# Two chunks of a retention kernel change places, four of their loads move to ScalarE's queue, and half of a block of gates moves ahead of the last output weights

## The chip, the cores and the metric

The kernel runs on one core of a Trainium2 chip. Its time is the device time of one execution in microseconds; the median of nine executions is given where nothing else is said. Lower is better.

## The reference

Causal retention over 8 sequences of 576 tokens with 8 heads of 64, and behind it a gated feed-forward layer on the 4608 tokens that come out.

```python
scores = (1 / sqrt(D)) * q @ k.T                          # per batch and head
gamma  = 1 - 2 ** (-5 - arange(H));  rel = pos[:, None] - pos[None, :]
ret    = scores * where(rel >= 0, gamma ** rel, 0)
x      = (ret @ v)                                        # then heads side by side: [4608, 512]
out    = (sigmoid(x @ w_gate) * (x @ w_val)) @ w_out      # 512 -> 1536 -> 512
```

## The kernel before

The sequences are cut into chunks of 128 tokens; the fifth chunk of each sequence has 64. There are 40 chunks, numbered from 0 in the order of tokens. Chunks 0 to 3 are done in pairs at the very start. Each later chunk s goes through these steps: its k, q and v are loaded (`load`), cast on GpSimd, called POOL here (`cast_k`, `cast_q`, `cast_v`, with the decay in the tables), turned by TensorE (`turn`, for chunks 4 and 5) or by a DMA transpose (`cross`, from chunk 6 on) into the tile `T`, and attended: a score step `qk` (L427) masked on VectorE (`pt`, L429), two state steps `st0` and `st1` (L460) whose sum VectorE copies to `sbd` (L466), and `pv` (L446, L448), which ScalarE copies into `xT` (L450). Chunk 4, `PAIRED`, is the short last chunk of sequence 0: it has `qk` and `pv` alone and uses the state that the pairs left. Chunk 5 is the first of sequence 1 and needs no earlier state. So neither depends on the other. `cast_dense` makes a second copy of v on ScalarE for the state steps.

The feed-forward layer runs over blocks of tokens. `h_units` makes, for each of 12 pieces `fc` of the 1536 hidden columns, the gate and value products on TensorE (L524), the sigmoid on ScalarE (`g`) and the product on VectorE (`gv`). Then `gv` times the output weights `wo_sb` gives `op`. A block of at most 256 tokens takes several pieces to one bank of PSUM; the banks come from a list given by the caller.

The change lies in the first 70 us, where the weights themselves are still being loaded. The first block is tokens 0 to 511 (`h_first`, called for each piece), with the four output banks `opps` and the 48 matmuls of L746; then comes the block of tokens 512 to 639, made of chunk 4 (64 tokens) and half of chunk 5. Both are written out by hand, and calls of `advance` put the attention steps of the list `order` between the matmuls. From token 640 on a loop does this by a count of columns.

Every engine works through its instructions in the order in which the program issues them, and so does SyncE's queue of loads. All loads go through 18 buffers `ld`; the list `freed` says by hand which earlier buffer a new load takes over. In the queue before stand the two pairs, the gate and value weights, chunks 4 and 5, output weights 0 to 7, chunk 6, output weights 8 to 11, chunk 7, and so on. `cast_wo(f, engine)` casts output weight f on the engine given; the cast waits for its load, and what is behind it on that engine waits too. Chunk 4 is loaded by six DMAs, two for each of k, q and v, one for the even and one for the odd heads on 64 partitions each.

Of the kernel before, what the change touches and what calls it, by code (L numbers as in the profile page):

```python
# [9 lines left out]
FP32 = mybir.dt.float32  # L10
# [6 lines left out]
def kernel(  # L17
# [59 lines left out]
    freed += [(nm, 0, i) for nm in "gv" for i in range(2)] + [("g", f, i) for f in (2, 4) for i in range(2)]  # L77
    freed += [("v", 2, 0), ("v", 2, 1), ("v", 4, 0), ("g", 6, 0), ("v", 4, 1), ("g", 6, 1), ("v", 6, 0), ("g", 8, 0),
              ("v", 6, 1), ("g", 8, 1), ("g", 10, 0), ("v", 8, 0), ("g", 10, 1), ("v", 8, 1), ("v", 10, 0), ("v", 10, 1)]
    freed += [("k", 4), ("q", 4), ("v", 4), ("o", 0), ("k", 5), ("o", 1), ("q", 5), ("o", 2), ("o", 3), ("o", 4), ("o", 5),  # L80
              ("o", 6), ("v", 5)] + [("o", f) for f in range(7, NFC)]
    for s in range(6, NS):
        freed += [("k", s), ("q", s)] + ([("v", s - 2)] if s > 7 else [])
    slot = {}
# [1 line left out]
    def ld_tile(shape, key):  # L86
        n = len(slot)
        slot[key] = n if n < SLOTS else slot[freed[n - SLOTS]]
        return ld_pool.tile(shape, FP32, tag=f"ld{slot[key]}", name="_".join(["ld"] + [str(x) for x in key]))
# [8 lines left out]
    def bank(psum, tag, shape, name, dt=FP32):  # L98
        if psum is ffn_psum:
            return ffn_bank(shape, name, dt)  # L100
        return psum.tile(shape, dt, tag=tag, name=name)

    def load(s):
        b, c = STEPS[s]
        n = width[c]
        t0 = c * P
        tiles = []
        for nm, src in (("k", k), ("q", q), ("v", v)):
            if s == PAIRED:

                t = ld_tile([P, M, D], (nm, s))
                for e in range(2):
                    nc.sync.dma_start(out=t[e * 64:e * 64 + 64], in_=src[b, e::2, t0:t0 + n, :].rearrange("m p d -> p m d"))
                tiles.append(t)
                continue
            t = ld_tile([P, H, D], (nm, s))
            nc.sync.dma_start(out=t[0:n], in_=src[b, :, t0:t0 + n, :].rearrange("h p d -> p h d"))  # L117
            tiles.append(t)
        loaded[s] = tiles

    def load_pair(A):
# [19 lines left out]
    def load_wo(f):  # L141
        t = ld_tile([P, DM], ("o", f))
        nc.sync.dma_start(out=t, in_=moe_w_out[f * P:(f + 1) * P, :])
        parts["o", f] = t
# [2 lines left out]
    load_pair(1)  # L147
    for f in range(0, NFC, 2):
        load_w(f, 2)
    load(4)  # L150
    load(5)
    for f in range(NFC):
        if f == 8:
            load(6)
        load_wo(f)
    LEAD_CAST = 3


# [31 lines left out]
    qtab, ktab = tables([P, NC, H, 1], [[P, NC], [1, 1]], 1, lambda t, h: t[:, :, h, :])  # L190
    qtab = qtab.rearrange("p c h o -> p c (h o)")
    ktab = ktab.rearrange("p c h o -> p c (h o)")

    qtab4, ktab4 = [consts.tile([P, M], FP32, name=nm) for nm in ("qtab4", "ktab4")]
    for t4, t in ((qtab4, qtab), (ktab4, ktab)):
        for hh in range(2):
            nc.vector.tensor_copy(out=t4[hh * 64:hh * 64 + 64], in_=t[0:64, NC - 1, hh::2])
    warm = consts.tile([P, 1], FP32)
    nc.scalar.activation(out=warm, in_=lnscale, func=AF.Sigmoid)

# [36 lines left out]
    def cast_wo(f, eng):  # L237
        eng(out=wo_sb[:, f, :], in_=parts.pop(("o", f)))
# [19 lines left out]
    def cast_k(s):  # L258

        b, c = STEPS[s]  # L260
        n = width[c]
        k32 = loaded[s][0]
        kn = qk_nat[s % NB][:, 1:3]
        for j in range(n // 64):
            for hh in range(2):
                nc.gpsimd.tensor_tensor(  # L266
                    out=kn[half(hh), j, :, half(hh)], in0=k32[half(hh)] if s == PAIRED else k32[half(j), hh::2, :],
                    in1=(ktab4[half(hh)] if s == PAIRED else ktab[half(j), c, hh::2]).unsqueeze(2).to_broadcast([64, M, D]),
                    op=ALU.mult)
        natural["k", s] = kn  # L270

    def cast_q(s):
        b, c = STEPS[s]
        n = width[c]
        q32 = loaded[s][1]
        if s == PAIRED:
            for hh in range(2):
                nc.gpsimd.tensor_tensor(
                    out=qk_nat[s % NB][0:n, 0, :, half(hh)], in0=q32[half(hh)],
                    in1=qtab4[half(hh)].unsqueeze(2).to_broadcast([64, M, D]), op=ALU.mult)  # L280
            return
        qs = qk_nat[s % NB][:, 0].rearrange("p m (hh d) -> p (m hh) d", d=D)
        nc.gpsimd.tensor_tensor(out=qs[0:n], in0=q32[0:n],  # L283
                                in1=qtab[0:n, c, :].unsqueeze(2).to_broadcast([n, H, D]), op=ALU.mult)

    def cast_v(s):

        b, c = STEPS[s]
        n = width[c]
        v32 = loaded[s][2]  # L290
        vb = vbd[s % NB]
        for j in range(n // 64):
            for hh in range(2):
                nc.gpsimd.tensor_copy(out=vb[half(hh), j, :, half(hh)],  # L294
                                      in_=v32[half(hh)] if s == PAIRED else v32[half(j), hh::2, :])
        natural["vb", s] = vb

    def cast_dense(s, j):
# [17 lines left out]
    def turn(s, engs):  # L316

        nb = 1 + width[STEPS[s][1]] // 64
        t = att_pool.tile([P, 3, M, P], BF16, tag="T", name=f"T_{s}", bufs=4)
        for b0, eng in zip(range(0, nb, 2), engs):  # L320
            n = min(2, nb - b0)
            ps = qk_psum.tile([P, n, M, P], BF16, tag="qk", name=f"Tp_{s}_{b0}")
            for i in range(n):
                for m in range(M):
                    nc.tensor.matmul(ps[:, i, m, :], lhsT=qk_nat[s % NB][:, b0 + i, m, :], rhs=ident,
                                     is_transpose=True, start=(i == 0 and m == 0), stop=(i == n - 1 and m == M - 1))
            eng(out=t[:, b0:b0 + n], in_=ps)
        turned["q", s] = t[:, 0]
        turned["k", s] = t[:, 1:3]

    turned = {}

# [5 lines left out]
    def half(x):  # L338
        return slice(x * 64, x * 64 + 64)
# [129 lines left out]

    order = []  # L470
    for s in range(PAIRED, NS):
        if STEPS[s][1] < NC - 1:
            order += [("st0", s), ("qk", s), ("st1", s), ("pv", s)]
        else:
            order += [("qk", s), ("pv", s)]
# [8 lines left out]
    def casts_to(s):  # L484
        while done["cast"] <= min(NS - 1, s):
            x = done["cast"]
            loads_to(x + (1 if x < 16 else 2))
            cast_k(x)
            cast_q(x)
            cross(x)  # L490
            cast_v(x)
            done["cast"] += 1

    def run_phase(kind, s):
        if kind == "qk":
            casts_to(s + LEAD_CAST)
            phase_qk(s)
            if s > 5:
                cast_dense(s + 1, 0)
        elif kind == "pv":  # L500
            phase_pv(s)
            if s > 5:
                cast_dense(s + 1, 1)
        else:
            phase_st(s, int(kind[2]))
# [120 lines left out]
    def h_first(fcs, a, e):  # L626
        run(h_units(gvs, fcs, 0, a, e))
# [71 lines left out]
    next_w(2)  # L699
    h_first((1,), 2 * P, 4 * P)  # L700
    for f in range(2, NFC, 2):
        h_first((f,), 0, 4 * P)
        next_w(f + 2)
        if f == 8:
            for s in (4, 5):
                cast_k(s)
                cast_q(s)
                cast_v(s)
        if f == 10:
            cast_wo(0, on_dve)  # L710
            turn(4, [on_act])
        h_first((f + 1,), 0, 4 * P)
        if zero:
            nc.vector.memset(zero.pop(0), 0.0)
    done["cast"] = 6
    loads_to(7)
    casts_to(6)
    at = 0
    cast_wo(1, on_act)
    advance(at + 1)  # L720
    cast_wo(2, on_dve)

    opps = [bank(ffn_psum if nb < 3 else tr_psum, "tr", [P, 512], f"op_0_{nb}") for nb in range(4)]
    cast_wo(3, on_act)
    for fc in range(NFC):
        if fc == 1:
            cast_wo(4, on_dve)
        if fc == 2:
            advance(at + 1)
            cast_dense(5, 0)  # L730
            cast_dense(5, 1)
            cast_wo(5, on_act)
            cast_wo(6, on_dve)
            cast_wo(7, on_act)
            cast_wo(8, on_dve)
        if fc == 4:
            turn(5, [on_act, on_dve])
            cast_wo(9, on_act)
            cast_wo(10, on_dve)
            cast_wo(11, on_act)  # L740
        if fc in (5, 6, 7, 9):
            advance(at + 1)
        if fc in (9, 11):
            cast_dense(6, (fc - 9) // 2)
        for nb in range(4):
            nc.tensor.matmul(opps[nb], lhsT=gvs[fc][:, nb * P:(nb + 1) * P], rhs=wo_sb[:, fc, :],  # L746
                             start=(fc == 0), stop=(fc == NFC - 1))
    for nb in range(4):
        store(opps[nb], nb * P, 1 + nb, on_dve if nb % 2 else on_act)
    gvs2 = {}  # L750
    for i, _ in enumerate(h_units(gvs2, range(NFC), 512, 0, P, [(qk_psum, "qk")] * 2 + [(ffn_psum, "ffn")] * 3 + [(tr_psum, "tr")])):
        if i in (3, 6, 8, 10):
            advance(at + 1)
    opp = ffn_bank([P, 512], "op_512")
    for fc in range(NFC):
        if fc == 6:
            advance(at + 1)
        nc.tensor.matmul(opp, lhsT=gvs2[fc], rhs=wo_sb[:, fc, :], start=(fc == 0), stop=(fc == NFC - 1))  # L758
    store(opp, 512, 2)
# [48 lines left out]
```

## Time and profile before

| | |
|---|---|
| median of 9 runs | 340.7 us (339.58 to 340.97) |
| profiled execution | 340.88 us, span of the instructions 339.2 us |
| TensorE busy | 326.9 us (96%), granted clock 0.989 on average |
| POOL, ScalarE, VectorE busy | 183.5, 172.7, 169.6 us |
| h matmuls of L524, gate and value | 117.8 + 118.4 us |
| first output weights, L746, on TensorE | 43.5 to 59.1 us |
| loads of output weights | 12 of 256 KB, 5.0 us from issue to landing (median) |

Busy time on TensorE is modelled at the end of each matmul and overlaps the next, so holes are found from the starts. "Idle before, releaser" in a row is the time that an engine stood still ahead of an instruction and what ended it. In SyncE's rows the length is the time that the queue took to issue, with no bytes moved yet.

### The profile page before, as it was taken

How to read it: one execution, taken by the hardware profiler on the slowest of the kernel's cores; microseconds unless marked ns; L12 is line 12 of the kernel's file. 1: busy time of each engine (PE TensorE's matmuls, PEld its weight loads, DVE VectorE, ACT ScalarE, POOL GpSimd, SP SyncE). 2: the span in 40 equal slices, each digit the busy share in tenths (PEclk: the TensorE clock that was granted, in tenths of full speed). 3: DMA queues.
4: the chain of work that ended last, by engine and by line, in shares of the span. 5: the costliest groups of instructions: out<-in, count | busy, mean ns of one | idle time of the engine just before them, and what ended most of it. 6: DMA issues, size and time to landing. Idle time of an engine off the chain costs nothing.

```text
span 339.2 us, 7564 instructions
## 1 busy us (share of the span) xinstructions
PE 326.9 (96%) x2828; PEld 188.8 (56%) x2860; DVE 169.6 (50%) x357; ACT 172.7 (51%) x355; POOL 183.5 (54%) x328
## 2 busy tenths in 40 slices
PE   7899987999999999999999999999999999999996
PEld 3574443898766556556556655544555455544443
DVE  6838624774646536516536625641664166503320
ACT  6635564566654556455455655454545455323321
POOL 7634847868878685794449975581659400000000
PEclk9959999999999999999999999999999999999999
DMA  7999999999999999999959999992994520020002
GB/s 209 313 348 291 251 290 217 152 216 189 211 196 263 181 256 254 198 267 198 172 147 196 206 181 262 177 176 104 230 201 85 140 65 0 2 93 31 2 31 93
DMA packets 169764, 60.13 MB, mean 177 GB/s; under 512 B 151168, under 2 KB 163712, under 8 KB 169728
## 3 DMA queue, kind: packets, MB, share of 16 engines
q1 hardware_dynamic: 169584, 59.52, 85.5%
q8 instruction: 22, 0.36, 0.5%
q14 instruction: 14, 0.11, 0.1%
q10 hardware_dynamic: 144, 0.13, 0.1%
HBM read 37.75 MB, written 9.44 MB: 139 GB/s over the span
## 4 chain that ended last, share of the span: by engine, by line
PE 88%; SPq 4%; DMA 3%; issue 2%; DVE 1%; ACT 1%; POOL 0%
PE h L524 54%; PE op L592 23%; SPq L126 2%; PE pv L448 2%; PE qk L427 2%; PE pv L446 2%; PE st L460 2%; DMA ld_g<-in_moe_w_gate_dram 2%; DMA ld_o<-in_moe_w_out_dram 2%; PE op L746 1%; PE op L582 1%; PE op L758 1%; PE pvp L410 0%; SPq L117 0%; DVE sbd L466 0%
## 5 line engine op out<-in xcount | busy, mean ns | idle before, releaser
L524 PE MATMUL h<-xT,wg_sb 128*128 128x512 bf16 (+3 forms) x575 | 117.8, 325 | 1.2 <-POOL wg_sb L233 0.6
L524 PE MATMUL h<-xT,wv_sb 128*128 128x512 bf16 (+3 forms) x579 | 118.4, 326 | 0.3
L266 POOL TENSOR_TENSOR qk_nat<-ld_k,ktab 64x256 bf16<-64x256 f32 x128 | 78.3, 612 | 55.1 <-PE st L460 27.3
L554 DVE TENSOR_TENSOR gv<-g,h 128x512 bf16<-128x512 bf16 (+1 forms) x106 | 66.4, 626 | 66.6 <-PE h L524 52.6
L550 ACT ACTIVATE g<-h 128x512 bf16<-128x512 f32 (+1 forms) x106 | 58.2, 549 | 73.6 <-PE h L524 66.4
L592 PE MATMUL op<-wo_sb,gv 128*128 128x512 bf16 x345 | 81.6, 379 | 0.8
L524 PEld LDWEIGHTS <-wg_sb 128*128 128x128 bf16 x584 | 51.8, 99 | 37.6 <-POOL wg_sb L233 0.9
L466 DVE CAST sbd<-st 64x256 bf16<-64x256 f32 x112 | 47.0, 420 | 47.2 <-PE st L460 44.6
L524 PEld LDWEIGHTS <-wv_sb 128*128 128x128 bf16 x584 | 51.3, 99 | 33.3
L294 POOL CAST vbd<-ld_v 64x256 bf16<-64x256 f32 x128 | 50.7, 396 | 11.8 <-PE pv L448 6.8
L592 PEld LDWEIGHTS <-gv 128*128 128x128 bf16 x360 | 33.2, 98 | 35.2
L305 ACT CAST vs<-ld_v 64x256 bf16<-64x256 f32 x112 | 45.1, 403 | 1.8
L564 ACT COPY ob<-op 128x512 f32<-128x512 f32 x33 | 19.2, 585 | 44.3 <-PE op L592 38.6
L283 POOL TENSOR_TENSOR qk_nat<-ld_q,qtab 128x512 bf16<-128x512 f32 (+1 forms) x35 | 36.4, 1041 | 3.2 <-DMA ld_q<-in_q_dram 0.5
L429 DVE TENSOR_TENSOR pt<-qk,tri 128x512 bf16<-128x512 f32 (+1 forms) x36 | 22.7, 629 | 17.5 <-PE qk L427 17.0
L450 ACT CAST xT<-pv 128x512 bf16<-128x512 f32 (+1 forms) x36 | 19.3, 537 | 21.8 <-PE pv L448 21.7
L460 PEld LDWEIGHTS <-qk_nat 128*128 128x128 bf16 x224 | 14.0, 98 | 10.2 <-issue 0.9
L448 PE MATMUL pv<-pt,vbd 128*128 128x64 bf16 x256 | 19.2, 193 | 0.0
L448 PEld LDWEIGHTS <-vbd 128*128 128x128 bf16 x256 | 16.2, 98 | 3.7
L446 PE MATMUL pv<-T,sbd 128*128 128x64 bf16 x228 | 18.1, 193 | 0.1
L446 PEld LDWEIGHTS <-sbd 128*128 128x128 bf16 x228 | 15.8, 98 | 2.5
L427 PEld LDWEIGHTS <-T 128*128 128x128 bf16 x256 | 12.3, 98 | 8.1 <-issue 2.1
(74 smaller groups left out, 177.0 us busy)
## 6 DMA issues: line engine op xcount, KB each, us to landing
out_dram<-ob SPq DMA_DIRECT2D x35, 256.0 KB, 2.4
ld_k<-in_k_dram SPq DMA_DIRECT2D x28, 256.0 KB, 4.2
ld_q<-in_q_dram SPq DMA_DIRECT2D x28, 256.0 KB, 4.6
ld_v<-in_v_dram SPq DMA_DIRECT2D x28, 256.0 KB, 5.0
ld_g<-in_moe_w_gate_dram SPq DMA_DIRECT2D x12, 256.0 KB, 6.0
ld_v<-in_moe_w_val_dram SPq DMA_DIRECT2D x12, 256.0 KB, 6.1
ld_o<-in_moe_w_out_dram SPq DMA_DIRECT2D x12, 256.0 KB, 5.0
ld_k_pair<-in_k_dram SPq DMA_DIRECT2D x4, 256.0 KB, 4.5
```

What stands on the lines that cost most here:

```text
L266: nc.gpsimd.tensor_tensor(out=kn[half(hh), j, :, half(hh)], in0=k32[half(hh)] if s == PAIRED else k32[half(j), hh::2, :], in1=(ktab4[half( ...
L283: nc.gpsimd.tensor_tensor(out=qs[0:n], in0=q32[0:n], in1=qtab[0:n, c, :].unsqueeze(2).to_broadcast([n, H, D]), op=ALU.mult)
L294: nc.gpsimd.tensor_copy(out=vb[half(hh), j, :, half(hh)], in_=v32[half(hh)] if s == PAIRED else v32[half(j), hh::2, :])
L305: nc.scalar.copy(out=natural["vs", s][half(hh), j], in_=loaded[s][2][half(j), hh::2, :])
L429: nc.vector.tensor_tensor(out=pt[:, :, 0:n].rearrange("p m (j t) -> p m j t", t=64), in0=qkp[:, :, 0:n].rearrange("p m (j t) -> p m j t", ...
L446: nc.tensor.matmul(pvp[:, m, half(j)], lhsT=before[:, m, :], rhs=qT[:, m, half(j)], start=True, stop=False)
L448: nc.tensor.matmul(pvp[:, m, half(j)], lhsT=vb[:, j, m, :], rhs=pt[:, m, half(j)], start=before is None, stop=True)
L466: nc.vector.tensor_copy(out=sb[half(hh), :, half(hh)], in_=st_tiles[b][half(hh)])
L524: nc.tensor.matmul(out, lhsT=w_sb[:, kc, fc * P:(fc + 1) * P], rhs=xT[:, kc, t0 + a:t0 + e], start=(kc == 0), stop=(kc == NKC - 1))
L550: nc.scalar.activation(out=g[:, 0:n], in_=h1[:, 0:n], func=AF.Sigmoid)
L554: nc.vector.tensor_tensor(out=gvs[some[0]][:, a:e], in0=g[:, 0:n], in1=h2[:, 0:n], op=ALU.mult)
L592: nc.tensor.matmul(opp, lhsT=gvs[fc][:, nb * P:(nb + 1) * P], rhs=wo_sb[:, fc, :], start=(fc == 0), stop=(fc == NFC - 1))
```

## The change

- Chunk 5 is loaded, cast, turned and attended ahead of chunk 4. The order of steps becomes st0 5, qk 5, st1 5, qk 4, pv 5, pv 4, with other places for the calls of `advance`.
- q of chunk 5 and all of chunk 4 are loaded from ScalarE's queue, k and v of chunk 5 from SyncE's. The calls stand in the loop of the first block: chunk 5 ahead of piece 6, chunk 4 ahead of piece 8, followed there by the output weights and chunk 6 (on SyncE's queue still).
- Chunk 4 is loaded by three DMAs in the form of all other chunks; its own tables `qtab4` and `ktab4` (four small VectorE copies) and its own forms of casts go. Its turned tile takes a buffer of the output pool.
- v of chunk 5 is copied on ScalarE ahead of activation 11, where chunk 4 was turned; chunk 5 is turned behind piece 11, and the cast of output weight 0 comes after that.
- The 48 matmuls of L746 are split: output weights 0 to 7, then the gates and values of six of the twelve pieces of tokens 512 to 639, then output weights 8 to 11. The casts of 8 to 11 are issued behind those six pieces.

```diff
-    freed += [("k", 4), ("q", 4), ("v", 4), ("o", 0), ("k", 5), ("o", 1), ("q", 5), ("o", 2), ("o", 3), ("o", 4), ("o", 5),
-              ("o", 6), ("v", 5)] + [("o", f) for f in range(7, NFC)]
+    freed += [("k", 5), ("q", 5), ("v", 5), ("o", 0), ("o", 1), ("k", 4), ("q", 4), ("v", 4)]
+    freed += [("o", f) for f in range(2, NFC)]
...
+    on_second = [("q", 5), ("k", 4), ("q", 4), ("v", 4)]
...
-            nc.sync.dma_start(out=t[0:n], in_=src[b, :, t0:t0 + n, :].rearrange("h p d -> p h d"))
             tiles.append(t)
+            (nc.scalar if (nm, s) in on_second else nc.sync).dma_start(
+                out=t[0:n], in_=src[b, :, t0:t0 + n, :].rearrange("h p d -> p h d"))
...
-    load(4)
-    load(5)
-    for f in range(NFC):
-        if f == 8:
-            load(6)
-        load_wo(f)
...
-        if STEPS[s][1] < NC - 1:
+        if s == PAIRED:
+            order += [("st0", 5), ("qk", 5), ("st1", 5), ("qk", 4), ("pv", 5), ("pv", 4)]
+        elif s == PAIRED + 1:
+            continue
+        elif STEPS[s][1] < NC - 1:
...
-            casts_to(s + LEAD_CAST)
+            casts_to(7 if s < 6 else s + LEAD_CAST)
...
     for f in range(2, NFC, 2):
+        if f == 6:
+            load(5)
+        if f == 8:
+            load(4)
+            for i in range(NFC):
+                if i == 8:
+                    load(6)
+                load_wo(i)
         h_first((f,), 0, 4 * P)
         next_w(f + 2)
         if f == 8:
-            for s in (4, 5):
+            for s in (5, 4):
...
         if f == 10:
-            cast_wo(0, on_dve)
-            turn(4, [on_act])
+            cast_dense(5, 0)
+            cast_dense(5, 1)
         h_first((f + 1,), 0, 4 * P)
...
+    turn(5, [on_act, on_dve])
...
     at = 0
+    cast_wo(0, on_dve)
     cast_wo(1, on_act)
     advance(at + 1)
...
+    def op_first(fcs):
+        for fc in fcs:
+            if fc == 1:
+                advance(at + 1)
+                cast_wo(4, on_dve)
+            if fc == 2:
+                turn(4, [on_act])
+                cast_wo(5, on_act)
+                cast_wo(6, on_dve)
+                cast_wo(7, on_act)
+            if fc in (3, 4, 5, 6):
+                advance(at + 1)
+            if fc == 7:
+                casts_to(8)
+            if fc in (9, 11):
+                cast_dense(6, (fc - 9) // 2)
+            for nb in range(4):
+                nc.tensor.matmul(opps[nb], ...)
+    op_first(range(8))
+    units2 = h_units(gvs2, range(NFC), 512, 0, P, [(qk_psum, "qk")] * 4 + [(ffn_psum, "ffn")] * 2)
+    for i in range(6):
+        next(units2)
+        if i == 5:
+            cast_wo(8, on_dve)
+    cast_wo(9, on_act)
+    cast_wo(10, on_dve)
+    cast_wo(11, on_act)
+    op_first(range(8, NFC))
     for nb in range(4):
         store(opps[nb], nb * P, 1 + nb, on_dve if nb % 2 else on_act)
-    for i, _ in enumerate(h_units(gvs2, range(NFC), 512, 0, P, [(qk_psum, "qk")] * 2 + [(ffn_psum, "ffn")] * 3 + [(tr_psum, "tr")])):
-        if i in (3, 6, 8, 10):
+    for i, _ in enumerate(units2):
+        if i in (2, 4):
             advance(at + 1)
     opp = ffn_bank([P, 512], "op_512")
     for fc in range(NFC):
-        if fc == 6:
+        if fc in (2, 6, 10):
             advance(at + 1)
```

More of the change, by code (lines that the diff above doesn't have):

```diff
@@ L108, in load @@
         for nm, src in (("k", k), ("q", q), ("v", v)):
[L109 to L115, printed above, removed]
             t = ld_tile([P, H, D], (nm, s))
-            nc.sync.dma_start(out=t[0:n], in_=src[b, :, t0:t0 + n, :].rearrange("h p d -> p h d"))
             tiles.append(t)
+            (nc.scalar if (nm, s) in on_second else nc.sync).dma_start(
+                out=t[0:n], in_=src[b, :, t0:t0 + n, :].rearrange("h p d -> p h d"))
         loaded[s] = tiles
@@ L192 @@
     ktab = ktab.rearrange("p c h o -> p c (h o)")
[L194 to L197, printed above, removed]
     warm = consts.tile([P, 1], FP32)
@@ L266, in cast_k @@
                 nc.gpsimd.tensor_tensor(
-                    out=kn[half(hh), j, :, half(hh)], in0=k32[half(hh)] if s == PAIRED else k32[half(j), hh::2, :],
-                    in1=(ktab4[half(hh)] if s == PAIRED else ktab[half(j), c, hh::2]).unsqueeze(2).to_broadcast([64, M, D]),
-                    op=ALU.mult)
+                    out=kn[half(hh), j, :, half(hh)], in0=k32[half(j), hh::2, :],
+                    in1=ktab[half(j), c, hh::2].unsqueeze(2).to_broadcast([64, M, D]), op=ALU.mult)
         natural["k", s] = kn
@@ L275, in cast_q @@
         q32 = loaded[s][1]
[L276 to L281, printed above, removed]
         qs = qk_nat[s % NB][:, 0].rearrange("p m (hh d) -> p (m hh) d", d=D)
@@ L293, in cast_v @@
             for hh in range(2):
-                nc.gpsimd.tensor_copy(out=vb[half(hh), j, :, half(hh)],
-                                      in_=v32[half(hh)] if s == PAIRED else v32[half(j), hh::2, :])
+                nc.gpsimd.tensor_copy(out=vb[half(hh), j, :, half(hh)], in_=v32[half(j), hh::2, :])
         natural["vb", s] = vb
@@ L318, in turn @@
         nb = 1 + width[STEPS[s][1]] // 64
-        t = att_pool.tile([P, 3, M, P], BF16, tag="T", name=f"T_{s}", bufs=4)
+        t = (att_pool.tile([P, 3, M, P], BF16, tag="T", name=f"T_{s}", bufs=4) if nb == 3
+             else osb_pool.tile([P, 2, M, P], BF16, tag="osb", name=f"T_{s}"))
         for b0, eng in zip(range(0, nb, 2), engs):
@@ L328, in turn @@
         turned["q", s] = t[:, 0]
-        turned["k", s] = t[:, 1:3]
+        turned["k", s] = t[:, 1:nb]
     turned = {}
@@ L724 @@
     cast_wo(3, on_act)
[L725 to L734, printed above, removed]
-            cast_wo(8, on_dve)
[L736 to L747, printed above, removed]
+    def op_first(fcs):
[15 more added lines that the diff above has]
+            for nb in range(4):
+                nc.tensor.matmul(opps[nb], lhsT=gvs[fc][:, nb * P:(nb + 1) * P], rhs=wo_sb[:, fc, :],
+                                 start=(fc == 0), stop=(fc == NFC - 1))
+    op_first(range(8))
+    gvs2 = {}
+    units2 = h_units(gvs2, range(NFC), 512, 0, P, [(qk_psum, "qk")] * 4 + [(ffn_psum, "ffn")] * 2)
+    for i in range(6):
+        next(units2)
+        if i == 5:
+            cast_wo(8, on_dve)
+    cast_wo(9, on_act)
+    cast_wo(10, on_dve)
+    cast_wo(11, on_act)
+    op_first(range(8, NFC))
     for nb in range(4):
         store(opps[nb], nb * P, 1 + nb, on_dve if nb % 2 else on_act)
-    gvs2 = {}
-    for i, _ in enumerate(h_units(gvs2, range(NFC), 512, 0, P, [(qk_psum, "qk")] * 2 + [(ffn_psum, "ffn")] * 3 + [(tr_psum, "tr")])):
-        if i in (3, 6, 8, 10):
+    for i, _ in enumerate(units2):
+        if i in (2, 4):
             advance(at + 1)
```

## The prediction, before the changed kernel ran

> **What bounds the kernel now.** I read the chain of waits first, since it tells which engine the end hangs on, and then the timelines of the stretch that the change touches.
>
> ```profile
> PE 88%; SPq 4%; DMA 3%; issue 2%; DVE 1%; ACT 1%; POOL 0%
> ```
>
> TensorE carries the end, so a change is worth what it adds to or takes from TensorE's own idle time. TensorE's timeline for 41 to 60 us shows where it stands still (start, length, engine, line, operation, count, idle time before and its releaser). Matmul ends are modelled, so I go by starts: a 512-column matmul takes 0.216 us (in "54.41 1.89 ... x7" seven start within 1.73 us, with one record missing), a 128-column one 0.056, a 64-column one 0.029.
>
> ```profile
> 41.21 0.61 PE L325 MATMUL Tp<-ident,qk_nat 128*128 128x128 bf16 x8
> ...
> 43.50 0.59 PE L746 MATMUL op<-wo_sb,gv 128*128 128x512 bf16 x2
> 44.40 1.46 PE L746 MATMUL op<-wo_sb,gv 128*128 128x512 bf16 x6 [0.30 <-DVE gv L554]
> ...
> 49.30 1.03 PE L746 MATMUL op<-wo_sb,gv 128*128 128x512 bf16 x4
> 52.41 0.39 PE L427 MATMUL qk<-T 128*128 128x64 bf16 x8 [2.08 <-DVE T L327]
> 52.64 1.03 PE L746 MATMUL op<-wo_sb,gv 128*128 128x512 bf16 x4
> 54.30 0.28 PE L460 MATMUL st<-vs,qk_nat 128*128 128x64 bf16 x4 [0.63 <-DVE sbd L466]
> ```
>
> There are three holes. The second matmul of the output projection starts at 43.72 and the third at 44.40: 0.68 - 0.22 = **0.46**. Four start from 49.30 and are through at 50.16, the next starts at 52.41: **2.25**. Four from 52.64 are through at 53.50, the next starts at 54.30: **0.80**. Together 3.5 us; from 54.30 to the end I find no hole over 0.3 us that isn't a missing record. VectorE's timeline names the cause:
>
> ```profile
> 45.57 0.43 DVE L238 CAST wo_sb<-ld_o 128x512 bf16<-128x512 f32 x1 [0.22 <-DMA ld_o<-in_moe_w_out_dram]
> 51.51 0.52 DVE L238 CAST wo_sb<-ld_o 128x512 bf16<-128x512 f32 x1 [5.51 <-DMA ld_o<-in_moe_w_out_dram]
> 51.95 0.41 DVE L327 COPY T<-Tp 128x512 bf16<-128x512 bf16 x1
> 52.82 0.65 DVE L238 CAST wo_sb<-ld_o 128x512 bf16<-128x512 f32 x1 [0.46 <-DMA ld_o<-in_moe_w_out_dram]
> 53.39 0.86 DVE L466 CAST sbd<-st 64x256 bf16<-64x256 f32 x2
> ```
>
> VectorE stands 5.5 us in front of the cast of output weight 8, whose load hasn't landed. The copy of chunk 5's transposes, long ready, is queued behind it, and TensorE waits for that copy; the third hole is the same with weight 10 and the state cast. SyncE's queue tells why it is late:
>
> ```profile
> 32.74 0.38 SPq L117 DMA_DIRECT2D ld_k<-in_k_dram  x1
> ...
> 42.67 3.39 SPq L117 DMA_DIRECT2D ld_v<-in_v_dram  x1
> 46.15 2.29 SPq L143 DMA_DIRECT2D ld_o<-in_moe_w_out_dram  x4
> ```
>
> Weights 8 to 11 are issued at 46.15 behind chunk 6. The DMA engines show 0.9 or more in every 2 us from 26 to 56, so the loads are bound by DMA throughput.
>
> [...]
>
> **The change part by part.**
> 1. *Output weights 8 to 11 needed later.* 24 gate and value groups of four 128-column matmuls (the timeline has one each 0.223 us) exist either way; twelve of them now run between output weights 7 and 8: 12 x 0.223 = 2.7 us. The casts that wait for 8 to 11 come after those matmuls, and no attention copy stands behind a missing weight. The weights landed at 51.5 to 53.6 before; TensorE asks for number 8 at about 56. Holes two and three go: -3.05 us.
> 2. *The first hole.* It waits for the last gv product to free a PSUM bank. Now chunk 5's 12 transposes (12 x 0.056 = 0.67) and a state step (0.11) stand ahead of the projection and cover it: -0.46. What is late next is weight 0. Its cast was done at 42.6 and is now emitted behind the transposes' copy. ScalarE: activation 10 to 41.15, four casts of chunk 5's v at 0.41 (moved ahead of activation 11) to 42.8, activation 11 to 43.4. VectorE: gv product 0.69 to 44.1, copy 0.41 to 44.5, cast 0.42 to 44.9. TensorE starts block 11 at 41.21 (chunk 4's eight transposes no longer stand there), ends it at 42.94, transposes and state step to 43.7. New hole: 44.9 - 43.7 = **+1.2**, at least 0.5 (were VectorE's rows to overlap and activation 11 not late), at most 2.0.
> 3. *Behind it.* Score step of chunk 5 at 45.8 (its ScalarE copy ends at 44.6: free); chunk 4's transposes at 47 (POOL's casts below); pv of 4 follows pv of 5 after one projection group (0.86), which covers the 0.59 copy that frees the pv bank. Three pairs of 128-token groups share two score banks: pair 3 waits for the gv product of pair 1, +0.25 by the latencies seen at 60 us; casts of weights 8 and 9 come right behind their pair's work, +0.3 and +0.15. Sum **+0.7**, 0 to 1.5.
> 4. *Loads.* Same bytes. Chunk 4 goes from six 64 KB loads to three of 128 KB; moved bytes fall to 145 GB/s at 32 to 34 us while these run (347 at 26 to 28), so up to 1 us may come back. SyncE's queue has 8 loads fewer, and chunk 5's k and v leave at 27.9, not 32.7. ScalarE issues q of chunk 5 after activation 5 (32.5) and three loads of chunk 4 after activation 7 (36.0). SyncE's rows for this size take 0.4 to 0.9 each; ScalarE is idle 1.13 before activations 6 and 8, so one is hidden, and three (1.2 to 2.7) delay activation 8 from 37.1 to 37.2-38.7; TensorE needs that activation done at 38.6, so 0 to 0.7, and I take 0. POOL's casts for chunk 5 then start at about 35 to 36, those of chunk 4 end at about 44: before their use at 47. Taken: loads 0, bounds -1 to +3.
> 5. *Dropped or bent.* Four small VectorE copies at 3.5 to 4.9 us go, hidden by the q load behind them (ended 6.2). Chunk 4's T takes an output buffer, of which there are 13, ten taken so far: 0. POOL's q cast of chunk 4 is one of 1.04 and not two of 0.68: hidden by POOL's wait for chunk 6 (3.9 us).
>
> Sum: -3.5 + 1.2 + 0.7 = -1.6 at TensorE. **Does it last?** Ahead of it lie the DMA transposes of later chunks. Time from landing to use was 2.7, 4.5, 2.5, 2.0, 2.0 and 1.57 us for chunks 6 to 11 (the last landing at 87.10, used at 88.67), then 5.7 and more. So with loads as before at most 1.57 lasts. I take -1.4. The profiled execution took 340.88 us (span 339.2 and 1.7 around it), 0.2 above the median of the nine runs, 340.7; the forecast is 339.5 against the one and **339.3** against the other.
>
> **The rivals.** What a measurement of this kernel can tell from no change is about 0.2%, 0.7 us.
> *Larger gain:* loads pack 1 us better, so chunk 11 allows 2.5, and the new hole is 0.5: -2.5, 338.2. For it speaks the 145 GB/s dip; against, 256-byte packets stay.
> *No change:* the wait for weight 0 at its bound of 2.0 and 1.2 behind it give back 3.2 of 3.5: 340.4. Or ScalarE's loads gain nothing and delay activation 8. VectorE's strict order speaks for it.
> *Slower:* completion counters. The trace shows eight in rotation: each SyncE load waits for the landing of the load eight before (weight loads are 0.75 us apart and land in 6.0). If ScalarE's loads share the rotation, weight 3 waits for q of chunk 5 and weights 5, 6, 7 for chunk 4's three, and SyncE holds chunk 6 and all later loads behind them. Weight 7 was issued at 40.6. If chunk 4's v lands later than that by d, every later load is late by d, and at chunk 11 the kernel loses d - 1.57: slower by 0.7 from d = 2.3 (a landing after 42.9). With d = 3: +1.4, **342.1**. Against it: issue at 36 to 38 and a landing time of 3.5 to 6 us for such small loads give 40 to 43; for it, ScalarE's issue can come late.
>
> **How the numbers follow.** Forecast 0.42, larger gain 0.18, no change 0.17, slower 0.23. Faster is the sum of the first two. The likeliest case alone spans 338.7 to 340.0; a tenth is left out at each end for 338.0 to 342.0.
>
> **What would show it.** Right: no VectorE wait of 5 us for ld_o, no hole of 2 us at the score step; one of about 1.2 us before the first projection matmul, with a VectorE cast of weight 0 ending it; the first blocks of tokens 640 on 1 to 2 us earlier; transposes of chunks 8 to 11 just in time. Wrong: TensorE waiting for T of chunks 8 to 11 from a DMA, SyncE held at weights 3 to 7, chunk 6's k landing after 49.5 (before 47.5), or activation 8 after 38.7.

## The result, and the profile after

The changed kernel took **345.56 us** (median of 10 runs) against 340.51 for the kernel before (32 runs in the same comparison): ratio 1.0149, 95% interval 1.013 to 1.0168, so 5.1 us slower. One of the ten runs, 350.83 us at a mean clock of 0.966, is a slow one, and the ratio leaves it out. The forecast was 339.3 us, with a range of 338.0 to 342.0. The profiled execution took 345.36 us, its span is 343.6; before it was 340.88 and 339.2, so the traces differ by 4.4 us in the span.

The head of the chain of waits, after the change. TensorE still carries the end, and two entries are new: ACTq and DVEq, time in which the sequencers of ScalarE and VectorE themselves stand in the chain.

```profile
PE 87%; SPq 3%; DMA 3%; DVE 2%; issue 2%; ACT 1%; ACTq 1%; POOL 0%; DVEq 0%
```

TensorE's waits after the change (waiting line, releaser: us in total, times, longest) have the loss in one row. Before, the longest was the 2.1 us of the score step for T; it is gone, and with it what the change was to remove.

```profile
PE h L508 <- ACT g L534: 6.9, 2, 5.5
PE op L737 <- DVE wo_sb L224: 1.2, 2, 1.0
```

TensorE's timeline after the change (start, length, engine, line, operation, count, idle time before and its releaser):

```profile
31.07 1.03 PE L508 MATMUL h<-xT,wg_sb 128*128 128x512 bf16 x4
33.45 1.02 PE L508 MATMUL h<-xT,wv_sb 128*128 128x512 bf16 x4 [1.36 <-ACT g L534]
...
36.04 1.03 PE L508 MATMUL h<-xT,wg_sb 128*128 128x512 bf16 x4
42.61 1.87 PE L508 MATMUL h<-xT,wv_sb 128*128 128x512 bf16 x4 [5.54 <-ACT g L534]
44.26 1.91 PE L508 MATMUL h<-xT,wg_sb 128*128 128x512 bf16 x4
...
47.25 1.03 PE L508 MATMUL h<-xT,wg_sb 128*128 128x512 bf16 x4
...
50.98 1.02 PE L737 MATMUL op<-wo_sb,gv 128*128 128x512 bf16 x4 [1.05 <-DVE wo_sb L224]
...
62.65 3.61 PE L737 MATMUL op<-wo_sb,gv 128*128 128x512 bf16 x15 [0.16 <-DVE wo_sb L224]
```

By starts, four matmuls of 0.216 each, there are two new holes: 33.45 - 31.93 = 1.52, and 42.61 - 36.90 = **5.71**. Behind the second the matmuls themselves are slow: twelve from 42.61 to 47.25 take 4.64 and not 2.59. The windows of 2 us say why (window, length; busy time and count of PE, PEld, DVE, ACT, POOL; granted TensorE clock; DMA share; GB/s):

```profile
38.00:40.00 2.00, 0.00 (x0) 0.00 (x0) 0.00 (x0) 0.00 (x0) 1.65 (x5) 0.99 1.05 388
40.00:42.00 2.00, 0.00 (x0) 0.00 (x0) 0.00 (x0) 0.04 (x1) 0.00 (x0) 0.50 1.20 300
42.00:44.00 2.00, 1.39 (x4) 0.56 (x4) 1.03 (x2) 1.56 (x3) 0.00 (x0) 0.50 1.38 140
44.00:46.00 2.00, 2.00 (x7) 0.63 (x5) 0.69 (x1) 0.00 (x0) 0.00 (x0) 0.50 1.39 174
```

The clock is halved, from 40.0 to 46.8: the half clock set in 3.1 us into the 5.7 us of idleness and lasted 6.8 us.

ScalarE's timeline after the change names who was late:

```profile
28.68 0.60 ACT L534 ACTIVATE g<-h 128x512 bf16<-128x512 f32 x1 [0.62 <-PE h L508]
32.27 0.43 ACTq L114 DMA_DIRECT2D ld_q<-in_q_dram  x1
32.81 0.60 ACT L534 ACTIVATE g<-h 128x512 bf16<-128x512 f32 x1 [3.53 <-DMA ld_v<-in_moe_w_val_dram]
...
39.36 0.69 ACTq L114 DMA_DIRECT2D ld_k<-in_k_dram  x1
40.15 0.67 ACTq L114 DMA_DIRECT2D ld_q<-in_q_dram  x1
40.91 0.60 ACTq L114 DMA_DIRECT2D ld_v<-in_v_dram  x1
41.96 0.60 ACT L534 ACTIVATE g<-h 128x512 bf16<-128x512 f32 x1 [7.55 <-DMA ld_o<-in_moe_w_out_dram]
```

The four loads leave ScalarE at 32.27 and from 39.36 on, and the two activations behind them stand 3.5 and 7.6 us. The releasers are landings of loads that have no data for these activations: a value weight and an output weight. The chain of waits, in order of time (start, us, what), shows the link:

```profile
33.45 5.90 DMA ld_o<-in_moe_w_out_dram
39.34 0.02 issue
39.36 0.69 ACTq L114
```

Output weight 2 lands at 39.34, and 0.02 us later ScalarE issues k of chunk 4. The trace records for each load the number of the completion counter on which its landing is counted. SyncE's and ScalarE's loads take turns on the same eight, 101 and 103 to 109:

| issued by ScalarE | at | counter | last used by | which landed at |
|---|---|---|---|---|
| q of chunk 5 | 32.27 | 104 | value weight of piece 10 | 32.21 |
| k of chunk 4 | 39.36 | 101 | output weight 2 | 39.34 |
| q of chunk 4 | 40.15 | 104 | q of chunk 5 | 36.92 (free) |
| v of chunk 4 | 40.91 | 105 | output weight 4 | 40.70 |

The waits that ScalarE holds ahead of these issues name the same counters. Ahead of k of chunk 4 it waits for 101 alone, so that load doesn't wait for the buffer that it takes over. The order on a counter is not that of the source, where chunk 4 stands ahead of the output weights.

**The ledger of the 4.4 us.** The first projection matmul starts at 50.98, before at 43.50: +7.48. Of that: holes 1.52 + 5.71 = +7.23; half clock +2.05; the hole in front of it, 49.76 to 50.98, +1.22; transposes and state step moved there, +0.2; and -3.15 that the change doesn't own: the profiled execution of before had its clock halved from 17.7 to 24.6, so its first 512-column matmul of the second piece started at 25.59, not 22.44. These terms add to 7.55, within 0.1 of the 7.48. From the projection to the end -3.1.

### The profile page after: what moved, and what is told of

Its sections match the earlier page's. It is cut to its first block, busy times and chain, and to the rows that moved or that the text cites. A ratio compares the mean times of both kernels' runs of the same rounds, so it can differ in the third digit from the quotient of the medians.

```text
span 343.6 us, 7549 instructions
## 1 busy us (share of the span) xinstructions
PE 326.8 (95%) x2827; PEld 187.9 (55%) x2860; DVE 168.9 (49%) x353; ACT 172.5 (50%) x355; POOL 184.1 (54%) x327
## 3 DMA queue, kind: packets, MB, share of 16 engines
HBM read 37.75 MB, written 9.44 MB: 137 GB/s over the span
## 4 chain that ended last, share of the span: by engine, by line
PE 87%; SPq 3%; DMA 3%; DVE 2%; issue 2%; ACT 1%; ACTq 1%; POOL 0%; DVEq 0%
PE h L508 51%; PE op L576 22%; PE op L737 3%; SPq L123 2%; PE pv L427 2%; PE qk L406 2%; PE pv L425 2%; PE st L439 2%; DMA ld_o<-in_moe_w_out_dram 2%; DMA ld_g<-in_moe_w_gate_dram 2%; PE op L566 1%; DVE gv L538 1%; SPq L140 1%; PE op L761 1%; ACTq L114 1%
## 5 line engine op out<-in xcount | busy, mean ns | idle before, releaser
L262 POOL TENSOR_TENSOR qk_nat<-ld_q,qtab 128x512 bf16<-128x512 f32 (+1 forms) x36 | 37.5, 1041 | 2.9
L439 PE MATMUL st<-vs,qk_nat 128*128 128x64 bf16 x224 | 15.7, 193 | 0.1
```

The costliest lines, as they stand in the source:

```text
L262: nc.gpsimd.tensor_tensor(out=qs[0:n], in0=q32[0:n], in1=qtab[0:n, c, :].unsqueeze(2).to_broadcast([n, H, D]), op=ALU.mult)
L439: nc.tensor.matmul(st_tiles[b][:, m, :], lhsT=natural["k", s][:, j, m, :], rhs=natural["vs", s][:, j, m, :], start=(c == 0 and j == 0 and ...
```

## The experiments

My theory after the result: ScalarE's issue of a load waits for the counter's last user to land, a landing set by SyncE's weights; the activations queued behind wait with it, and TensorE after them. Rivals are the reverse order itself; the issue time of the loads on ScalarE; more DMA traffic. Ratios are to the kernel before on the same chip; runs of before had medians of 340.5 to 341.05.

**e1: all loads back on SyncE**, the rest of the change kept.

```
-    on_second = [("q", 5), ("k", 4), ("q", 4), ("v", 4)]
+    on_second = []
```

> The changed kernel with all loads back on SyncE's queue (the list on_second is empty). Theory A (ScalarE stands at each of its own load issues until the load eight before has landed and frees the completion counter, so activations 6 and 8 behind it are late and TensorE stands still for 1.5 and 5.7 us, after which its clock is halved for 6.8 us): both holes and the late slow stretch go, about 338 us (337 to 339.5). Theory B (the loads themselves land late or disturb each other, whoever issues them): chunk 4 lands late still, at 343 to 345. Theory C (the new order and the split of the output weights cost the time, by the wait for output weight 0 and the score banks): no change, 345.

Measured 338.32 us, ratio 0.9935 (0.9911 to 0.9959): 7.2 us below the changed kernel, 2.2 below before. TensorE's waits on the projection and on the transposes in e1, and its only late transposes:

```profile
PE op L737 <- DVE wo_sb L224: 2.5, 2, 2.1
...
PE qk L406 <- DMA T<-qk_nat: 0.2, 1, 0.2
```
```profile
85.63 0.41 PE L406 MATMUL qk<-T 128*128 128x64 bf16 x8 [0.23 <-DMA T<-qk_nat]
```

Both holes at the gates are gone and the clock is full throughout. The whole loss sits in the four queue words; what is left of the change gains 2.2. As the loads and their bytes are the same, more DMA traffic as such isn't the cause. The first projection matmul starts at 42.85, 8.13 sooner than after the change; the end comes 7.4 sooner.

**e2: only q of chunk 5 on ScalarE. e3: only chunk 4's three.**

```
e2  +    on_second = [("q", 5)]
e3  +    on_second = [("k", 4), ("q", 4), ("v", 4)]
```

> The changed kernel with q of chunk 5 alone on ScalarE's queue, chunk 4 back on SyncE's. Theory A: only the wait ahead of activation 6 remains, a hole of about 1.5 us on TensorE, 339 to 340.5 us. Theory B: [...] most of the loss goes for lack of contention, 339 or less, with q of chunk 5 landing when it did. Theory C: 345.

> The changed kernel with the three loads of chunk 4 alone on ScalarE's queue, q of chunk 5 back on SyncE's. Theory A: the wait ahead of activation 8 remains, a hole of 4 to 6 us and the halved clock behind it: 343 to 344.5 us. Theory B: the same 343 to 345, but ScalarE's activation 8 would be on time (37 to 38 us). Theory C: 345.

e2: 339.08, ratio 0.9954 (0.993 to 0.9978). Its issue came at 32.37, behind a gate weight that landed at 32.31, but opened no hole, against theory A's 1.5: in the profiled execution the clock was halved from 19.6 to 23.0, and the activation ahead of the load came at 30.50 and not at 28.68. e2 stands 0.8 above e1, with intervals that overlap: one load alone costs little. e3: **345.62**, ratio 1.0143 (1.0117 to 1.0169): the three alone make the loss, with a hole of 7.4 us on TensorE; theory A had expected 4 to 6 us and 343 to 344.5. ScalarE's timeline in e3:

```profile
37.39 0.71 ACTq L114 DMA_DIRECT2D ld_k<-in_k_dram  x1
38.70 0.61 ACTq L114 DMA_DIRECT2D ld_q<-in_q_dram  x1
41.06 0.61 ACTq L114 DMA_DIRECT2D ld_v<-in_v_dram  x1
41.77 0.60 ACT L534 ACTIVATE g<-h 128x512 bf16<-128x512 f32 x1 [9.44 <-DMA ld_o<-in_moe_w_out_dram]
```

With q of chunk 5 back among SyncE's loads, ahead of the output weights, the rotation has moved on by one, and the partners are others: output weights 0, 2 and 4, landed at 37.29, 38.63 and 40.96. Each issue follows within 0.1 us. The issues themselves take 0.6 to 0.7 each, 1.9 together; the rest of the 9.44 is the wait. That refutes the rival of issue time.

**e4: the four loads from GpSimd.**

```
-            (nc.scalar if (nm, s) in on_second else nc.sync).dma_start(
+            (nc.gpsimd if (nm, s) in on_second else nc.sync).dma_start(
```

> The changed kernel with the same four loads issued from POOL instead of ScalarE, at the same places of the program. POOL has slack there (it waits for chunk 5's k) and no activation stands behind a load. Theory A: 338 to 339.5 us, unless POOL's own wait delays its casts by more than their slack of some 3 us. Theory B: the loads are still apart from SyncE's and still late, 343 to 345. Theory C: 345.

Measured 340.5, ratio 0.999 (0.9972 to 1.0009), above theory A's 338 to 339.5. In e4's trace GpSimd's loads are counted on counters of their own, 111 to 114. Its timeline:

```profile
26.82 1.07 POOL L114 DMA_DIRECT2D ld_q<-in_q_dram  x1
...
29.79 0.69 POOL L114 DMA_DIRECT2D ld_k<-in_k_dram  x1
30.48 0.68 POOL L114 DMA_DIRECT2D ld_q<-in_q_dram  x1
31.15 0.68 POOL L114 DMA_DIRECT2D ld_v<-in_v_dram  x1
```

They leave one behind the other, with SyncE's weights still on the way, and no activation is late. So a second queue isn't what costs 5 us; the shared counters are. But e4 is 2.2 above e1. Chunk 5's v landed at 40.0 (e1: 38.3), and the profiled execution had its clock halved from 13.0 to 26.7; all its 20 runs have a mean clock of 0.98 to 0.995 (e1: 0.99 to 1.0). Which of them makes the 2.2 stays open.

**e5: the second hole filled** with 24 matmuls on a blank tile, ahead of the value matmuls of piece 9.

```
+                if t0 == 0 and some[0] == 9:
+                    for x in range(2):
+                        warmp = qk_psum.tile([P, 512], FP32, tag="qk", ...)
+                        for y in range(12):
+                            nc.tensor.matmul(warmp, lhsT=blank[:, 0:P], rhs=blank, ...)
```

> The changed kernel with 24 matmuls on a blank tile (24 x 0.216 = 5.2 us, results unused, into two spare score banks) put on TensorE just ahead of the value matmuls of piece 9, where it stood idle for 5.7 us. Theory A1 (the hole costs twice: 5.7 us of standing and then 2.5 us because the clock is halved from 40.0 to 46.8 us): the clock stays up, 343 us (342.5 to 343.5). Theory A2 (the halved clock is hidden, since the loads set the pace until 50 us anyway): 345.5, no change.

Measured 343.83, ratio 1.0096 (1.0068 to 1.0123): 1.7 us back of the 2.05 that the ledger gives the clock. In its profile the clock was halved after all, from 34.0 to 37.5, behind the first hole, 2.3 us long here. So TensorE came late to the 24 matmuls, and they outlasted the wait: activation 8 was done at 42.93, and the value matmuls began at 44.29. The one run with a mean clock of 1.0 took 343.1, 2.5 below the changed kernel. The hole costs its own length, and the clock behind it about 2 us more.

**e6: the kernel before, with chunk 5's k, q and v issued by ScalarE** ahead of activation 8; no reverse order, no moved gates.

```
-            nc.sync.dma_start(out=t[0:n], ...)
+            (nc.scalar if s == 5 else nc.sync).dma_start(out=t[0:n], ...)
...
+        if f == 8:
+            load(5)   # and the output weights with chunk 6 behind it, as in the change
```

> The kernel before, in its own order and without the split, with k, q and v of chunk 5 issued from ScalarE's queue ahead of activation 8 and the output weights behind them on SyncE's. Theory A: ScalarE again stands for completion counters, activation 8 is late by 3 us or more, and the kernel is slower by 2 to 6 us (342.5 to 346). Theory C (the loss comes from the new order): within 1 us of 340.5.

Measured **345.21**, ratio 1.0135 (1.0108 to 1.0161). ScalarE's timeline in e6:

```profile
37.84 0.45 ACTq L117 DMA_DIRECT2D ld_k<-in_k_dram  x1
39.93 0.37 ACTq L117 DMA_DIRECT2D ld_q<-in_q_dram  x1
40.92 1.91 ACTq L117 DMA_DIRECT2D ld_v<-in_v_dram  x1
42.93 0.60 ACT L545 ACTIVATE g<-h 128x512 bf16<-128x512 f32 x1 [10.41 <-DMA ld_o<-in_moe_w_out_dram]
```

The same signature and the same loss without the rest of the change; TensorE's hole is 8.4 us, the half clock behind it 37.8 to 48.1. The reverse order isn't needed for the loss.

**What the rest of the change is worth.** Three edits of e1 and one of the kernel before. **e7**: e1, with weight 0's cast ahead of the copy that e1's 2.2 us hole waits behind, and chunk 5's v casts behind activation 11 and no longer ahead of it.

```
+            cast_wo(0, on_dve)      # behind piece 11, ahead of turn(5)
-    cast_wo(0, on_dve)              # behind turn(5)
...                                  # the two cast_dense(5, ...) stand behind piece 11
```

> All loads on SyncE's queue (as e1), and besides the cast of output weight 0 stands ahead of the copy of chunk 5's transposes on VectorE, and the copies of chunk 5's v behind activation 11 on ScalarE. The hole of 2.2 us ahead of the first output matmul should fall to about 1.0 (the weight lands at 41.1). If the DMA transposes of chunks 8 to 11 cap the gain, as their 0.05 to 0.9 us between landing and use in e1 say, the time stays at 338.3 (0.4 either way) and TensorE waits for the transposes instead. If not, 337.2.

Measured 338.31, ratio 0.9929 (0.991 to 0.9948): nothing was gained over e1's 338.32, so that hole wasn't what set the end. The profile shows less than the median: it is of an execution of 341.74 us with the clock halved from 13.5 to 27.2, in which TensorE came to the projection 5.4 us later than in e1. There the hole is 0.5 us and no transpose is late; what an execution at the median waits for wasn't seen.

**e8**: e1 without the split, with all twelve output weights before the gates of tokens 512 to 639, and the casts of 8 to 11 at weight 7.

```
-    op_first(range(8)) ... op_first(range(8, NFC))
+    op_first(range(NFC))            # at fc == 7: cast_wo(8) to cast_wo(11)
```

> All loads on SyncE's queue (as e1), without the split: the twelve output weights in one go, the casts of 8 to 11 issued behind weight 7, the gates and values of tokens 512 to 639 behind all. If the split is what hides the late weights, TensorE waits for weights 8 to 11 for 1.5 to 2.5 us, 339.8 to 341. If keeping their casts away from the attention copies is enough, the weights (landed at 50.0 to 52.6 in e1) are in time but for about 0.5 us: 338.3 to 339.

Measured 337.62, ratio 0.9927 (0.9898 to 0.9956). A hole of 1.2 us stands at weight 8 instead, and the end comes no later than in e1, below both expectations: the split isn't needed.

**e9**: e1 with the four small table copies back on VectorE.

```
+    for t4, t in ((qtab4, qtab), (ktab4, ktab)):
+        for hh in range(2):
+            nc.vector.tensor_copy(out=t4[hh * 64:hh * 64 + 64], in_=t[0:64, NC - 1, hh::2])
```

> All loads on SyncE's queue (as e1), with the four small VectorE copies of the tables put back (their results unused). The mean clock of e1's runs is 1.0 in most, that of the kernel before 0.995 or less in nearly all. If the copies, by delaying the start, cause the early halved clock, the clock falls to 0.99 to 0.995 and the time rises to 338.8 to 340. If not: 338.3 and the clock as in e1.

Measured 338.38, ratio 0.9929 (0.9906 to 0.9952), like e1: the copies are worth nothing, as forecast. In its profile TensorE waited 2.2 us for DMA transposes.

**e10: the kernel before, with nothing changed but the place of four casts.**

```
-            cast_wo(8, on_dve)            # at fc == 2; 9 to 11 at fc == 4
+        if fc == 7:                       # behind the attention step of fc == 7
+            cast_wo(8, on_dve)
+            cast_wo(9, on_act)
+            cast_wo(10, on_dve)
+            cast_wo(11, on_act)
```

> The kernel before, with the casts of output weights 8 to 11 alone moved: behind the attention step at weight 7, no longer ahead of and around the turning of chunk 5. If VectorE's wait for weight 8 in front of the copy of chunk 5's transposes is what the first two holes of the kernel before were (2.25 and 0.80 us), they go, a hole of about 1.2 us stays at weight 8 (landed 51.5), and the kernel gains 1.2 to 1.8 us, near 339.2. If the reversed order is needed for the gain, 340.5.

Measured **337.61**, ratio 0.9909 (0.9886 to 0.9932), 3.4 us below before, twice the expected 1.2 to 1.8, and the lowest median of all, level with e8's within the intervals. TensorE's timeline in e10:

```profile
49.05 0.81 PE L747 MATMUL op<-wo_sb,gv 128*128 128x512 bf16 x3
51.52 1.02 PE L747 MATMUL op<-wo_sb,gv 128*128 128x512 bf16 x4 [1.66 <-DVE wo_sb L238]
52.73 2.75 PE L747 MATMUL op<-wo_sb,gv 128*128 128x512 bf16 x12
```

Weight 8 still lands late, at 50.19, but only the weight's own matmuls wait: one hole of 1.6 us (three of four matmuls from 49.05 are recorded) in place of the two at the score step and the state step, and the clock stays full. Why it gains more than the two holes, the next run shows.

**e11: the kernel before once more**, for what its first profile, with its early half clock, hid.

> The kernel before once more, for a second profile of where its clock is halved. If by the hole of 2.2 us near 50 us, the slow window begins at 50 to 54 us; if by the start, at 12 to 20 us, as in the first profile.

One run, 341.42. TensorE's timeline and the windows in e11:

```profile
46.24 1.03 PE L746 MATMUL op<-wo_sb,gv 128*128 128x512 bf16 x4
51.34 0.59 PE L427 MATMUL qk<-T 128*128 128x64 bf16 x8 [4.07 <-DVE T L327]
```
```profile
48.00:50.00 2.00, 0.00 (x0) 0.00 (x0) 0.28 (x1) 0.00 (x0) 1.79 (x4) 0.89 1.03 347
50.00:52.00 2.00, 0.66 (x9) 0.53 (x9) 1.97 (x5) 0.62 (x1) 1.88 (x4) 0.50 1.19 305
52.00:54.00 2.00, 2.00 (x9) 0.82 (x8) 1.22 (x3) 0.62 (x1) 1.34 (x3) 0.50 1.37 219
```

Here TensorE was done with the weights ahead of the score step at 47.10 (50.16 in the first profile) and waited 4.2 us, up to 51.34 (52.41). Weight 8 landed at 49.70, its cast took 1.24 us and the copy followed; in the first profile these were 51.48 and 0.52. The clock is then half from 49.6 to 56.4. So the first profile showed 2.25 us of a hole that is 4.2 us when the start runs at full clock, and it brings the half clock with it. The mean clocks fit: 0.99 to 0.995 in all 11 runs of before beside e10, 1.0 in four of e10's six.

## Why the prediction was wrong, by its steps

**Step 4 is the one that failed.** It has ScalarE "issue" the four loads after activations 5 and 7 and lets them cost their own duration. That duration was right: the three took 0.69 + 0.67 + 0.60 = 1.96 us, within 1.2 to 2.7. What it had at nothing is the wait of an issue for its completion counter: the first of the three left at 39.36 and not at 36.0, and q of chunk 5, called hidden, opened 1.52 us. Activation 8 came at 41.96, past the 38.7 that the prediction named as a sign of being wrong. The term "0 to 0.7, and I take 0" measured 5.71 us; with the load called hidden it is 7.23 us of holes, and 2.05 of half clock behind them. The traces show ScalarE holding an issue until the counter's last user has landed, and all that is queued behind it with it: after the change k of chunk 4 left 0.02 us after output weight 2 had landed, and in e3 one activation stood 9.44 us behind three such issues. (A slip without effect: SyncE's queue has seven loads fewer, not eight.)

**The slower rival had the resource and the wrong victim.** It named the rotation of eight, but let SyncE wait for ScalarE's loads. SyncE issued eight output weights from 30.21 to 36.90 and k of chunk 6 at 37.67 (before 41.07), held by none of them; TensorE waited for no DMA transpose. It is ScalarE that waited for SyncE's loads, and ScalarE is the queue with a compute engine behind it. Its price, a late landing of chunk 4's v passed on to chunk 11, wasn't paid either, though that v landed as late as 49.1: the next loads on chunk 4's three counters left at 48.42 to 52.05, after those landings.

**Step 1** was right in mechanism: holes two and three went. From the projection on, where the three holes (-3.5), step 3 (+0.7) and the moved transposes (-0.2) put -3.0, the traces differ by -3.1. That it fits so well is partly luck, as the size came from a profile with an early half clock: in e11 the hole is 4.2 us, and the same stretch is 6.4 us longer than after the change. The means were more than needed: e10 has the gain from the casts' place alone, and e8 has it without moving the gates.

**Step 2** was right to 0.02 us in the changed kernel: 1.22 against 1.2. In e1 the same hole is 2.2, just above the upper bound of 2.0. VectorE's timeline in e1 shows why:

```profile
41.22 0.42 DVE L306 COPY T<-Tp 128x512 bf16<-128x512 bf16 x1
41.55 1.24 DVE L224 CAST wo_sb<-ld_o 128x512 bf16<-128x512 f32 x1
```

Weight 0 had landed at 41.12, before that copy was done, but its cast took 1.24 us and not 0.42; what stretched it stays open. In e2 and e8, with casts of 0.72 and 0.57, the hole is 1.3 and 1.2. **Step 3**, +0.7, was about right: the holes among the 128-token groups and at weight 8 are 0.27 and 0.32 after the change, 0.27 and 0.54 in e1. **Step 5**, nothing, held for the copies (e9).

**The cap held as a mechanism and was mis-sized.** The gain without ScalarE's loads was forecast at 1.4 and measured at 2.2 (e1), 3.1 in e8 and 3.4 in e10, whose intervals overlap. Chunk 11's transposes are used 0.05 us after landing in e1, e2, e8, e9 and e10, and from that use to the end every trace of this case takes 250.4 to 250.6 us: where TensorE is early enough, DMA transposes set the end. But I took their landing as fixed (87.10); in e1 it came at 85.58, in these five runs at 84.99 to 87.03. They had moved themselves, in e1 by 1.5 us. The larger-gain rival's 338.2 is what the change is worth without ScalarE's loads (338.32), partly by luck: its hole of 0.5 measured 2.2.

## What to carry to other kernels

A load issued from an engine that computes can hold that engine for a landing that has nothing to do with it (9.44 us in e3); before moving a load there, ask which completion counter it takes and when that counter's last user lands, or issue it where the counters are free, as GpSimd's were in e4 (340.5 us, no activation late). A cast that waits for a late load belongs behind everything on its engine that is ready, as the four casts of e10, which made the whole gain (3.4 us). A hole that ends at a fixed landing takes up whatever is gained ahead of it (2.25 us in one profile of before, 4.2 in the other), so its length in one profile is no measure of what its removal brings.

## What the hardware did that I had not expected

In these traces half clock came with long holes and cost more than a small hole (2.05 us in the changed kernel). Behind holes of 4.2 us (e11), 5.7 (after), 7.4 (e3) and 8.4 (e6) the clock was half for 6.8, 6.8, 6.8 and 10.2 us, behind one of 2.3 in e5 for 3.4; the holes of 1.2 to 2.2 in e1, e8 and e10 and that of 2.25 in the first profile of before had none behind them. These lengths are one, two or three times 3.41 us, and in each trace the changes of the clock lie on a grid of that width. What tells these cases apart is how much of one grid window the hole fills. In the changed kernel a border lies at 39.97, so the hole from 36.90 to 42.61 fills 90% of the window before it and 77% of the one behind, and the clock is half in the two windows that follow, 40.0 to 46.8. In e11, with a border at 49.57, the shares are 72% and 52%, again with two half windows. In the first profile of before the hole fills 50% of one window and 16% of the next, in e1 22% and 44%, and no half window follows. So in these traces behind the start a window filled by holes to 52% or more was followed by one at half clock, and none filled to 50% or less was; two holes of nearly one length (2.3 us in e5, 2.25 in before) differed by where the border fell.

Some executions also have half clock in the first 27 us (before 17.7 to 24.6, e2 19.6 to 23.0, e4 13.0 to 26.7, e7 13.5 to 27.2), and others of the kernel before (e11) and of e2 and e7 (mean clock 1.0) have none. There the share is no clear sign: in before's window ahead of 17.7 the holes (0.39, 0.35 and 0.81 us) fill about 45%, and only with every gap of about 0.1 us between matmuls is it over 52%. Why they come stays open. The grid doesn't start with the kernel's first instruction: counted from it, the borders fall 2.4 us past a multiple of 3.41 in the changed kernel and 0.7 us past one in before.
